# A new order for the same 1682 steps: memory attention mixed with a state-space convolution on one core

## The chip, the core and the metric

The kernel runs on one core of a Trainium2 chip. The core has five engines that matter here, each with an instruction list of its own that it works through strictly in order: PE (TensorE, the matmuls), ACT (ScalarE), DVE (VectorE), POOL (GpSimd) and SP (SyncE, which does nothing here but issue transfers). An engine stops at an instruction until everything that the instruction waits for has been signalled by the other engines or by a transfer. The metric is the time of one execution in microseconds (us) of the device. Data is bf16.

## The reference, cut to what matters

One input x, 2048 tokens of 512 features, goes through two branches, and a gate per token mixes them:

```
# branch A: 32 heads of 16, 4 segments of 512 tokens
for s in range(4):
    p     = softmax(qs @ ks^T / 4 + causal mask)        # inside the segment
    a_dot = p @ vs
    a_mem = (phi(qs) @ M) / (phi(qs) @ z + 1e-6)        # from the segments before
    o_s   = sigmoid(beta) * a_mem + (1 - sigmoid(beta)) * a_dot
    M    += phi(ks)^T @ vs;  z += sum(phi(ks))          # phi(t) = t+1 if t>0 else exp(t)
a = concat(o_s) @ wo
# branch B: K[d,l] = Re sum_n C[d,n] * exp(dt*A[d,n]*l) * (dt*B[d,n]);  causal convolution
b = irfft(rfft(pad(x)) * rfft(pad(K))) + x * Dskip
g = sigmoid(sum(x * gate_w))
out = g * a + (1 - g) * b
```

## The kernel before, in words

**Work.** The kernel is a list of 1682 steps, and a step is one vector or scalar instruction, one transfer, or a group of matmuls that belong together. Branch A is worked in 16 groups: 4 segments times 4 groups of 8 heads (`project`, `scores`, `ophase`). A group has five score tiles of 128x2048 or 128x1024, so there are 80 in all. For each, PE writes the scores into PSUM banks 0 to 3 (line 1108), ACT takes the exponential into SBUF (line 1132), and PE multiplies the result with the values. In the first two segments PE adds the causal mask as a matmul (line 1127), in the last two DVE multiplies by it (line 1145). `norm` (lines 1092 to 1099) divides by the sums. The score tiles all use the same four banks, so the scores of one tile cannot begin before the exponential of the one before has ended. All other results of PE go through the four banks 4 to 7, or through 0 to 3 between two score tiles.

**The convolution.** `ssm_prep` and `ssm_powers` compute exp(dt*A) and its squares up to the power 2^9 (ACT squares on line 824, copies from line 832). `tables` builds for each of four blocks of 128 features, in complex products on DVE (lines 1228, 1231, 1235 and `cmul1`), two tables of powers; the lag matmuls (line 1284, eight steps per table, named 1027 to 1030 and 1032 to 1035 for table 0, with the copies 1031 and 1036) make the convolution kernel K from them. The convolution itself is a transform in two levels: `x_level1` (steps 1215 to 1298) multiplies x by a 128-point transform and stores the result to DRAM, scr_Z, through a few SBUF tiles; `tail` reads it back, 2 halves times 16 frequencies, and multiplies it with the transform of K. `finals` adds both branches in PSUM, applies the gate in the last copy and stores the output.

**Copies.** Every result in PSUM that a later matmul needs is copied to SBUF. Most copies go through `S.evac` (line 224), which has two forms: ACT (line 226, or 229 with a factor) and DVE (227, or 230 with a factor). Which engine makes a copy is written in the order. There are 243 steps with such a choice.

**Queues.** Nearly all transfers are issued by SP, in its list's order (line 222, and line 724 for the transposing loads of x, steps 577 and 794 for segments 2 and 3). An issue occupies SP for a few tenths of a microsecond, a transposing one for longer. A step that issues a transfer waits on SP for its data, and the transfers behind it wait too.

**What sets the order.** The order of all steps is written out in full, in the string `ORDER` (lines 372 to 456). Each word is a step's number, then `a` where a copy goes to ACT (`v` or nothing: DVE), then the slots (PSUM banks or buffer numbers) that the tiles which begin their life there take:

```
1027/4/0      # step 1027 (first lag product of table 0); PSUM choice 4, buffer 0 of its pool
1240v         # step 1240, a copy, on DVE
```

For a tile of one bank the choices 0 to 7 stand for the banks 4, 5, 6, 7, 0, 1, 2, 3. `replay` (line 235) walks the words and appends each step to its engine's list; `emit` (line 264) then puts in the waits that the data and the reuse of buffers need, given that order. So one word in another place changes the lists of one engine, and the waits, but no instruction.

**Steps that the prediction names.** Start: 23 (an 8 KB load of beta), 36 (first exponential of `ssm_prep`), 189 (exponential of the gates, line 885). `x_level1`: 1217, 1219, 1222, 1224, 1240, 1250, 1253, 1255 (copies into the tiles that are stored to scr_Z), 1225, 1235, 1251 (stores). 106 is a square of `ssm_powers` (line 824), 157 and 175 are copies of a power to bf16 (line 832), 987, 1044, 1099 and 1102 copies of powers into the tables 0, 1 and 2 (line 226 or 227). 801 is the copy of a projection of segment 3. 1657 to 1664 are the last two output tiles.

Of the kernel before, what the change touches and what calls it, by code (L numbers as in the profile page):

```python
# [372 lines left out]
16/0 386/0 214/0 193/0 205/1 15/0 10/0 17/0 0/0 25/1/0 11/1 9/2 27/2 33/0 26 41/0 44/1 45 28 34/2 42/3 12/3 35/4  # L373
29/3/1 46 47 30a 1236/0 7/0 1239/0/0 1249/4/1 23/0 37/5 183/0 38 39 189/0 190 36/6 191 43/7 48/0 54/8 3/0 40 194 50/9
1240v 49/10 13/4 53/1 59/1 51/11 52 5/0 60/5 178/2 14/5 1250a 55/12 66/3 64/0 65 58/0 56/13 57 61a/0 62/1 63v 72/4
76/1 77/5 78 67a/0 68 91v/1 79v/2 31/6/2 32a 90/6 70/2 71 181/3 192/0 1247/2 1237/7 1238a 92 88/0 89 102/7 103v/3
1248a 82/1 83/1 184/2 104 100/0 80 101 1/0 19/0 200/3/0/0 201a 202 115v/4 292/0/1/1 84 293a 116 179/1 114/3 294 182/0
20/0 18/0 203/4/0 204a 22/0 372/0 180 208/1 209a 210/2 222/0/0 4/0 217/3/0/0 218 220 223 1215/1 212/0 112/0 113 186/3
213a 69 94/1 211a 373/1 127v/5 187 983v/0 374/0 206/0 185 224 207a 794/0 1251 1221/2/1 1222v 987v/0 128 8/0 219 126/5
1223/1 1224a 124/0 225/0/0 93 81 984v 105 991/0 992 125 988/1 986v 195 226 227 1241 136/3 138/6 137 96/2 139v/6 993  # L380
989 990 251/0/2/2 985v 252a 196/2 197 216 95 140 254/1/1 253 150/7 255a 117 151v/7 1225 998/0 387/3 388v 129 229/0/1
215 230 24 148/2 149 1218/0/0 1219a 231 1231/1/1 1232a 1233/0 1234v 381/2/2 1235 997 163v/8 237/0/2 238 999 106/0 239
389/1 390v 164 152 162/0 1001/1 994 108/3 141 375/0 228/3 232 233 234/0 241/0/0 242 198 199/0 382a 243 295/0/0 1216/2
1217a 1220 263/0/1 264 160/3 265 1252/1/1 1253a 296v 995/0 165 1000 161 153 1002 240/2 1254/0 1255a 244 270/0/1 188
271 996 272 245 795/1 796 172v/9 1256 235 236/0 393/0 266/0/0 267 394a 1003 246/1 268 1007/1 1006 247 1004/0 107 248
378/1/0/0 1008 379a 1244/3/0 1245a 278/0/2 279 280 1226/0/1 173 1005 174 269/1 273 1227a 274 275/2 1010/1 1009 276
1012 277/1 1242/3 1278/0 1243a 1246 385/0 1228/2 282/0/0 283 284 334/0/1 335a 309/0/1 310 1229a 1230 311 281/3 1011
1018 1019/0 1016/1 1020 221/0/0 256/2/0/0 257 259 258 1021 1013/0 331/1/2/2 332a 302/0/0 303 304 285 286 305/0/0 287/3
306 1015 288 118/1 119/5 260 577/0 307 261/0 1289/1/0 1281/2/1 317/0/2 318 1282a 289 1014 1022/0 1023 377/1 1024 1290a
319 1257/1 1025/0 120 1017 1026 132/6 1291/2 1292a 1047/1 1293 308/0 249/3 250a/0 380 297/1/0/0 312 313 314/4 1049/0  # L390
321/0/0 322 323 1046 333 315 435/2/1/1 1279/3 1027/4/0 1028 1280a 1029 1030 436a 1265/3/0 320/2 324 325 1263/5 130/2
131 437 316/0 298 300 299 1283 383/0 142/3 143/7 144 326/5 156/0 327 1032/0 384 1033 1034 1035 328 1050 262 1266a
1031a 154/0 1264a 155 1036a 1040/0 1037 343/0/1 1044v/0 73a/3 344 1038 1045v/0 1041a 1051 1042v 1055 1048 1056/0
1260/1/1 1267 1043a 6/0 345 350/0/1 1261a 109v/2 169a/0 1053/1 1057 1052 1058 351 352 1059/0 1054 85a/4 110 1060
1065/1 86 1064 170 1066 1061 1067 1068/0 1070 290/3 291a 74 1069 1258/2 1259a 1062/1 1076 1262 1063 1077/0 329/0
1273/1/0 346/0/0 347 348 1275/3 1276a 438/2/0 439a 362/0/2 363 330a 364 1268/3/1 1274a 1277 1269a 1270/2 349/0 353 354
355/0 358/0/0 359 360 87 1073 1078 356 1079 357/1 1080/1 391/1 1039 402/0/0 403 392a 395 1271a 1272 301/3 336/1/0/0
404 337 338 339 1074/0 361/2 1081 1071/1 405/0/1 145a/1 1075 1082 406 111 407 1083/0 171 1296/0/0 1297a 1072 340 166/1
75 365 366 396 409/0/0 410 411 408/1 133a/5 1084 483/0/2/2 397/4/0/0 398 400 399 367/1 134 1286/5/1 1294/6 1295a 1298
121a/6 122 123 157a/8 368 158 369 168/2 1105/1 1107/0 1284/7 1285a 1104 341 1108 167 146 412 175v/7 1287a 1288 159 413  # L400
1090/6/1 1091 1092 1093 1094a 401/2/1 417/0/2 418 135 484a 97a/9 98 443/0/0/0 444 414/2 176 99 177 485 445 147 446 415
342 419 416/0 1085/3 1086 1087 1088 1109/0 1103a 1114/0 1089a 1299/0 453/0/0 1097 454 455 1300/0 1098 1113 1307/1
1106/0 1115 1096 447 448 1116 1101a 486/0/1 1095 1100a 1306/1 1117/1 1099v 370/1 1118 421/0/1 1102a 1110 422 423
532/3/2 487a 529/2/0/0 1120/0 533a 450/0/1 1119 451 452 530a 420/0 1129/1 424 1121 425 426/3 371a 1317/2 1128 1301/3/0
1336/0 1132/0 1302a 1130 496/0/0 497 498 1303/2/0 1304a 1305/0 457/0/1 458 459 1310/1/1 1311a 578/3 579 1308/2/1 1309a
1312/1 1318/1 580 465/0/2 1111/1 466 427 456/1 460 467 461 1313/1/0 1314a 469/0/0 470 1112 428 471 1122 1324/0
# [1101 lines left out]
```

## Time and profile before

| | |
|---|---|
| median of 3 runs | 294.76 us (294.18, 294.76, 295.40) |
| the profiled execution | 294.76 us |
| its span in the profile | 293.0 us, mean granted TensorE clock 0.988 |
| PE busy | 254.9 us, 87% of the span |
| DVE busy | 257.9 us, 88% (641 instructions) |
| ACT busy | 254.0 us, 87% (314 instructions) |
| POOL busy | 5.2 us |
| weight loads on PE (overlapping) | 174.3 us |
| 80 exponentials of the scores (line 1132) | 137.0 us of ACT, 1713 ns on average |
| chain that ended last | PE 53%, ACT 30%, DVE 8%, issue 4%, DMA 3% |
| DMA | 41.83 MB, 143 GB/s on average; the queue that SP feeds took 49.3% |

The span is what the profiler saw of the execution, and the time is longer by what lies around it. Busy time counts an engine's instructions, not its waits. In a row of the timeline stand the start in us, the duration in us (of the whole run of equal instructions, where several stand together), the engine, the line of the code, the operation, the tiles and the form; in brackets the idle time of the engine ahead of it and what ended that idle time. "SPq" is SP's queue, "issue" idle time in which the engine waited for nothing that the profile shows. In a table by stretches each row gives a stretch of time, its length, then for each engine the busy time and how many instructions began in it, the granted clock of TensorE and what the transfers took. In the chain of waits a row gives only start, duration, engine, tile and line.

### The profile page before, as it was taken

Reading aid. Unit: us, or ns where it says so; the run is one execution under the profiler, and the core shown is the slowest. Engines: PE = TensorE matmul, PEld = TensorE weight load, DVE = VectorE, ACT = ScalarE, POOL = GpSimd, SP = SyncE. Lnnn points to the kernel's source line nnn. Section 1 sums busy time; section 2 is a strip of 40 time slices with the busy share of each in tenths; the row PEclk is TensorE's granted clock in tenths of the full one; section 3 lists DMA queues with packets and bytes.
Section 4 is the critical chain, followed back from the end, with each engine's and each line's share of the span. In section 5 each row is a group of like instructions: output and inputs, shape, how many; then the busy total and the mean of one; then the engine's idle time right before and its main releaser. Section 6 shows DMA issues by size and latency. Waiting matters only on the chain.

```text
span 293.0 us, 12663 instructions
## 1 busy us (share of the span) xinstructions
PE 254.9 (87%) x5623; PEld 174.3 (59%) x5665; DVE 257.9 (88%) x641; ACT 254.0 (87%) x314; POOL 5.2 (2%) x11
## 2 busy tenths in 40 slices
PE   3677888776777889999999979999999999999993
PEld 2333364546345657677777757777767777646662
DVE  3998999999999998999999969889988899787643
ACT  3998999998999999989999869898998899987630
POOL 5000000000000000000000000000000000000000
PEclk9999999999699999999999999999999999999999
DMA  6999331941314455506526546547657766421135
GB/s 178 305 175 196 86 102 39 213 123 41 92 53 103 120 142 169 192 21 199 153 76 189 135 157 171 201 142 237 207 158 218 223 192 204 130 74 40 38 74 144
DMA packets 45128, 41.83 MB, mean 143 GB/s; under 512 B 21009, under 2 KB 40466, under 8 KB 45074
## 3 DMA queue, kind: packets, MB, share of 16 engines
q1 hardware_dynamic: 43922, 40.47, 49.3%
q8 instruction: 44, 0.72, 1.0%
q10 hardware_dynamic: 1152, 0.56, 0.8%
q14 instruction: 10, 0.08, 0.1%
HBM read 25.88 MB, written 6.29 MB: 110 GB/s over the span
## 4 chain that ended last, share of the span: by engine, by line
PE 53%; ACT 30%; DVE 8%; issue 4%; DMA 3%; SPq 0%; ACTq 0%
PE psum L692 52%; ACT sb L1132 15%; ACT sb L226 9%; ACT sb L824 2%; DMA scr_Z<-sb 2%; DMA sb<-in_B_B_im_dram 1%; ACT sb L832 1%; DVE sb L1228 1%; DVE sb L1235 1%; DVE sb L1348 1%; DVE sb L1231 1%; ACT sb L983 1%; DVE sb L1099 1%; DVE sb L227 1%; DVE sb L1145 1%
## 5 line engine op out<-in xcount | busy, mean ns | idle before, releaser
L692 PE MATMUL psum<-sb 128*32 128x20 bf16 (+17 forms) x5535 | 248.2, 218 | 28.8 <-ACT sb L1132 11.2
L692 PEld LDWEIGHTS psum<-sb 128*128 128x128 bf16 (+8 forms) x5577 | 167.7, 99 | 106.4 <-issue 24.9
L1132 ACT ACTIVATE sb<-psum 128x2048 bf16<-128x2048 f32 (+1 forms) x80 | 137.0, 1713 | 12.4 <-PE psum L692 11.9
L226 ACT ACTIVATE sb<-psum 128x512 bf16<-128x512 f32 (+3 forms) x143 | 87.6, 651 | 9.9 <-PE psum L692 7.0
L227 DVE CAST sb<-psum 128x512 bf16<-128x512 f32 (+2 forms) x44 | 31.1, 715 | 7.6 <-PE psum L692 5.5
L1235 DVE TENSOR_TENSOR sb<-sb 128x512 bf16<-128x512 bf16 (+3 forms) x44 | 30.4, 698 | 0.2
L1231 DVE TENSOR_TENSOR sb<-sb 128x512 bf16<-128x512 bf16 (+3 forms) x44 | 30.4, 695 | 0.2
L1228 DVE TENSOR_TENSOR sb<-sb 128x512 bf16<-128x512 bf16 (+3 forms) x44 | 30.3, 696 | 0.0
L1348 DVE TENSOR_TENSOR sb<-sb 128x1024 bf16<-128x1024 bf16 x32 | 21.7, 686 | 2.2 <-ACT sb L226 2.0
L1145 DVE TENSOR_TENSOR sb<-sb 128x512 bf16<-128x512 bf16 (+1 forms) x40 | 18.1, 472 | 2.1 <-ACT sb L1132 2.0
L1099 DVE TENSOR_TENSOR sb<-psum,sb 128x256 bf16<-128x256 f32 x32 | 13.5, 421 | 0.4
L230 DVE TENSOR_SCALAR sb<-psum,sb 128x512 bf16<-128x512 f32 x9 | 6.7, 748 | 6.3 <-PE psum L692 6.2
L824 ACT ACTIVATE sb<-sb 128x512 f32<-128x512 f32 x18 | 11.4, 640 | 0.0
L229 ACT ACTIVATE sb<-psum,sb 128x512 bf16<-128x512 f32 x6 | 4.1, 686 | 6.2 <-PE psum L692 6.2
L1096 DVE RECIPROCAL sb<-psum 128x16 f32<-128x16 f32 x32 | 8.1, 253 | 1.3 <-PE psum L692 1.2
L1182 DVE TENSOR_TENSOR sb<-psum,sb 128x512 bf16<-128x512 f32 x12 | 8.3, 689 | 0.3
L1038 ACT ACTIVATE sb<-sb 128x512 bf16<-128x512 bf16 x12 | 7.7, 642 | 0.5 <-PE psum L692 0.4
L825 DVE TENSOR_TENSOR sb<-sb 128x256 f32<-128x256 f32 x18 | 7.6, 420 | 0.3 <-ACT sb L824 0.3
L983 ACT ACTIVATE sb<-psum 128x512 bf16<-128x512 bf16 x12 | 7.3, 610 | 0.3 <-PE psum L980 0.3
L826 DVE SCALAR_TENSOR_TENSOR sb<-sb 128x256 f32<-128x256 f32 x18 | 7.5, 416 | 0.0
L1097 DVE TENSOR_TENSOR sb<-sb 128x16 f32<-128x16 f32 x32 | 5.5, 172 | 0.4
L832 ACT ACTIVATE sb<-sb 128x512 bf16<-128x512 f32 x9 | 5.6, 635 | 0.0
(79 smaller groups left out, 116.8 us busy)
## 6 DMA issues: line engine op xcount, KB each, us to landing
sb<-c_DNM SPq DMA_DIRECT2D x32, 480.0 KB, 4.1
scr_Z<-sb SPq DMA_DIRECT2D x16, 256.0 KB, 2.9
sb<-scr_Z SPq DMA_DIRECT2D x32, 128.0 KB, 3.5
sb<-sb SPq DMA_DIRECT2D x32, 128.0 KB
sb<-in_A_x_dram SPq DMA_DIRECT2D x5, 512.0 KB, 5.0
sb<-sb SPq DMA_DIRECT2D x20, 64.0 KB, 3.2
out_dram<-sb SPq DMA_DIRECT2D x18, 64.0 KB, 1.8
sb<-sb SPq DMA_DIRECT2D x8, 136.0 KB, 3.8
```

Of the source, the lines that this page charges most:

```text
L226: fa = lambda e: e.activation(dst(), src(), ACT.Copy)
L227: fd = lambda e: e.tensor_copy(dst(), src())
L692: mm = lambda e, o_, l, r_, st, sp, **kw: e.matmul(o_, lhsT=l, rhs=r_, start=st, stop=sp, skip_group_check=True, **kw)
L824: op("ACT", ("As", 512), lambda e, sq=sq, Z=Z: e.activation(ap(sq, n=512), ap(Z, n=512), ACT.Square), r=[Z], w=[sq], key=PW[h] + PWS * k)
L983: op("ACT", ("Ax", 512), lambda e: e.activation(ap(ek, n=512), ap(P, n=512), ACT.Exp), r=[P], w=[ek])
L1099: op("DVE", ("V1", 256), lambda e: e.tensor_tensor(ap(o1, gi * 16, [[128, 4], [32, 4], [1, 16]]), ap(T, dims=[[68, 4], [17, 4], [1, 16]]), ...
L1132: o = op("ACT", ("Ax", 4 * w), lambda e, P=P, pT=pT, w=w: e.activation(ap(pT, dims=[[w, 4], [1, w]]), ap(P, dims=[[512, 4], [1, w]]), ACT. ...
L1145: op("DVE", ("V2", 1024 if ent is None else 512), lambda e, pT=pT, pd=pd, md=md: e.tensor_tensor(ap(pT, dims=pd), ap(pT, dims=pd), md(), A ...
L1228: op("DVE", ("V2" if n > 1 else "V1", 256 * n), lambda e: e.tensor_tensor(run(tile, ne, dst, 1), run(tile, ne, src, sstep), ap(pw, cl * 51 ...
L1231: op("DVE", ("V2" if n > 1 else "V1", 256 * n), lambda e: e.tensor_tensor(run(t2, n, 0, 1), run(tile, ne, src, sstep), ap(pw, cl * 512 + 2 ...
L1235: op("DVE", ("V2" if n > 1 else "V1", 256 * n), lambda e: e.tensor_tensor(D_(), D_(), ap(t2, n * 128, [[-n * 128, 2], [2 * n, 64], [1, 2 * ...
L1348: op("DVE", ("V2", 1024), lambda e, Y=Y, X=X, K3=K3: e.tensor_tensor(ap(Y, dims=[[512, 2], [256, 2], [1, 256]]), ap(X, dims=[[256, 2], [0, ...
```

## The change

Only the string `ORDER` is changed. The 1682 steps, their instructions, transfers, tiles and the memory for them are the same. The order of the words is another nearly everywhere, made from the old one by many small moves; on average a step stands 2 places from its old one in PE's list, 7 in ACT's, 10 in DVE's and 5 in SP's. 44 of the 243 copies change their engine: 28 go from DVE to ACT and 16 from ACT to DVE, so that ACT has 331 steps in place of 319 and DVE 629 in place of 641. Tiles take other slots here and there. The 80 exponentials stand in the same order as before.

Of the diff, which replaces all 83 lines of the string, these are the lines that hold the steps of the prediction (before, then after; whole lines):

```
...
-29/3/1 46 47 30a 1236/0 7/0 1239/0/0 1249/4/1 23/0 37/5 183/0 38 39 189/0 190 36/6 191 43/7 48/0 54/8 3/0 40 194 50/9
-1240v 49/10 13/4 53/1 59/1 51/11 52 5/0 60/5 178/2 14/5 1250a 55/12 66/3 64/0 65 58/0 56/13 57 61a/0 62/1 63v 72/4
...
-213a 69 94/1 211a 373/1 127v/5 187 983v/0 374/0 206/0 185 224 207a 794/0 1251 1221/2/1 1222v 987v/0 128 8/0 219 126/5
-1223/1 1224a 124/0 225/0/0 93 81 984v 105 991/0 992 125 988/1 986v 195 226 227 1241 136/3 138/6 137 96/2 139v/6 993
-989 990 251/0/2/2 985v 252a 196/2 197 216 95 140 254/1/1 253 150/7 255a 117 151v/7 1225 998/0 387/3 388v 129 229/0/1
-215 230 24 148/2 149 1218/0/0 1219a 231 1231/1/1 1232a 1233/0 1234v 381/2/2 1235 997 163v/8 237/0/2 238 999 106/0 239
...
-1217a 1220 263/0/1 264 160/3 265 1252/1/1 1253a 296v 995/0 165 1000 161 153 1002 240/2 1254/0 1255a 244 270/0/1 188
...
-306 1015 288 118/1 119/5 260 577/0 307 261/0 1289/1/0 1281/2/1 317/0/2 318 1282a 289 1014 1022/0 1023 377/1 1024 1290a
...
-321/0/0 322 323 1046 333 315 435/2/1/1 1279/3 1027/4/0 1028 1280a 1029 1030 436a 1265/3/0 320/2 324 325 1263/5 130/2
-131 437 316/0 298 300 299 1283 383/0 142/3 143/7 144 326/5 156/0 327 1032/0 384 1033 1034 1035 328 1050 262 1266a
-1031a 154/0 1264a 155 1036a 1040/0 1037 343/0/1 1044v/0 73a/3 344 1038 1045v/0 1041a 1051 1042v 1055 1048 1056/0
...
-121a/6 122 123 157a/8 368 158 369 168/2 1105/1 1107/0 1284/7 1285a 1104 341 1108 167 146 412 175v/7 1287a 1288 159 413
...
-1106/0 1115 1096 447 448 1116 1101a 486/0/1 1095 1100a 1306/1 1117/1 1099v 370/1 1118 421/0/1 1102a 1110 422 423
...
-619 620 628/0/1 629 535 536/0 621/1 543 605 645 694/0/0/0 695v 627/1 800/2/1/1 801v 630 606 607 622 696 623/0 663/0/2
...
-1622 1623v/2 962 966 1665/3 1657/0 970 1641/2 1669/4 976/3/1/1 963/1 967/1 971 972 1642 1658 1670 977 978 979 1666
-973/2 974 1643a 1653 1654 1655 1656 975 980 981/5 982a 1610/6 1659 1660v/3 1671 1667 1672/4 1673 1668a 1678 1679 1680
-1681 1601/1 1630/2 1602 1603v/5 1631 1632a 1633 1634 1635 1636 1611 1612v 1613 1614 1615 1616 1661/7 1662 1663 1664v
-1674 1675 1676 1677
+15/0 16/0 0/0 10/1 23/0 9/5 11/3 17/5 33/0 25/4/1 189/0 190 26 34/13 12/2 41/5 1236/1 27/0 37/0 28 35/10 36/1 38 7/0
...
+1250a 183/2 193/0 53/7 52 47 1240a 19/0 178/3 64/3 1237/6 66/1 1247/3 65 54/9 62/1 1238a 192/0 4/0 60/2 20/0 18/0
...
+136/3 1251 81 218 227 219 215 1221/0/1 229/0/0 220 137 148/3 388v 230 991/1 293a 389/3 129 1241 983v 216 24 1233/1/0
+140 984v 992 231 1222v 1223/2 72/1 381/0/1 1224a 184/2 294 987a/0 390v 237/0/2 150/5 1234v 238 151v/6 149 70/0 989/0
+577/0 386 993 382a 1231/2 375 228/3 232 233 71 234/5 254/0/2 988 1225 235 794/0 163v/8 187 239 1232a 1235 241/0/0 82/3
...
+995/1 378/3/2/0 999 996 296v 1255a 265 1216/0/0 96/4 270/0/1 271 1218/1 1253a 240/2 244 245 95 1217a 161/3 272 266/0/0
+267 1219a 1256 379a 268 162 1006 1228/0/1 1226/1 1007/0 393/3 278/0/2 246/0 394a 172v/9 1008 1227a 153 141 279 269/3
...
+256/0/0/0 1003 1278/1 1021 331/3/0/1 1230 106/1 1005 107 311 1012 302/0/0 120/6 332a 383/0 303 796 1246 257 304
...
+333 435/2/1/2 1050/1 314/0 1046/0 130/0 298 436a 322 315 323 1047 1283 1049 1027/3/1 132/0 1028 1293 1029 1030 1031a
+1032/2 316/1 300 1033 1034 131 1035 1036a 343/0/1 344 1051/0 1045v 1037/0 1042v/0 1041a 1260/3/0 320/0 1038 1044a
+1258/2 142/2 324 299 109v/7 325 97a/5 1263/1/1 1048 1055 98 99 73a/3 144/2 326/5 1043a 345 350/0/1 1264a 351 110 1259a
+74 1056/1 327 143 1057 328 1052 1265/1 111 1040 352 1053/1 346/0/0 157v/1 1058 347 1054 1059/0 1064 158 1065/1 156/3
...
+1102a/0 1336/1 448 1115 455 421/0/0 422 487a 1100a 1301/1/0 342 423 171 529/3/2/0 1116 450/0/1 1117/0 168 1118 424
+1302a 1306/2 1106 451 1120/0 371a 1101a 1096 452 1119 456/1 1095 1098 1307/0 1308/2/1 1129/1 1309a 425 1128 496/0/0
+497 1097 175a/6 1303/2/1 1318/0 498 426/4 457/0/0 530a 1304a 1121 458 459 532/3/1 1099a 1130 1310/2/0 1311a 1305/0
...
+615/3 1394a 619 1469/3 449 620 628/0/1 694/0/1/0 621/0 629 800/1/2/2 622 626 801a 627/2 1451/2 1444/0 607 1396/1
+663/0/2 623/0 664 695v 1206/3 697/0/1 630 631 632 696 667/0/0 1462/1 1407/2 802 1207 1208 1209 698a 571/0/3/0 1387 809
...
+1681 1630/5 1678 1679 1631 1632a 1611 1612v/3 1636 1635 1602 1603v 1613 1615 1661/0 1657/1 1614 1658 1616 1662 1659
+1634 1633 1660v/4 1663 1664a 1674 1677 1676 1675
```

129 lines of the change are left out of this document (64 added, 65 removed).

## The prediction, made before the time of the changed kernel was known

> **What bounds the kernel now.** I read the page's first lines, then the busy time by stretches, then the timeline with what ended each idle time.
>
> ```profile
> span 293.0 us, 12663 instructions
> PE 254.9 (87%) x5623; PEld 174.3 (59%) x5665; DVE 257.9 (88%) x641; ACT 254.0 (87%) x314; POOL 5.2 (2%) x11
> ```
>
> The sum is made on this execution: 294.76 us, span 293.0 and 1.76 us around it. It is also the median of the three runs (294.18 to 295.4). No engine is full over the whole, so I cut the span where the limit changes:
>
> ```profile
> core 0: us, PE busy (x) PEld busy (x) DVE busy (x) ACT busy (x) POOL busy (x), PEclk, DMA share, GB/s
> 7.28:25.05 17.77, 12.31 (x110) 6.65 (x112) 17.08 (x51) 17.71 (x35) 0.00 (x0) 1.00 1.14 228
> 25.05:41.12 16.07, 13.04 (x187) 6.33 (x189) 14.61 (x49) 14.99 (x22) 0.00 (x0) 1.00 0.44 117
> 41.12:118.68 77.56, 61.92 (x1711) 42.38 (x1724) 75.38 (x177) 74.90 (x98) 0.66 (x1) 0.96 0.39 109
> 110.00:118.68 8.68, 8.66 (x193) 6.57 (x192) 7.70 (x14) 7.85 (x9) 0.00 (x0) 1.00 0.42 140
> 118.68:170.00 51.32, 50.00 (x1233) 36.67 (x1238) 50.30 (x119) 47.63 (x60) 0.67 (x1) 1.00 0.47 141
> 170.00:180.00 10.00, 8.40 (x311) 5.66 (x311) 7.54 (x24) 7.07 (x8) 0.00 (x0) 1.00 0.49 163
> 180.00:285.00 105.00, 103.12 (x2000) 73.09 (x2015) 88.23 (x217) 88.50 (x94) 0.00 (x0) 1.00 0.51 154
> 285.00:293.00 8.00, 3.47 (x70) 1.90 (x69) 2.25 (x3) 0.69 (x1) 0.00 (x0) 1.00 0.55 145
> ```
>
> From 7.28 to about 110 ACT and DVE are both full while PE has holes. From 110 on PE is full: 8.66 of 8.68 us, then 50.00 of 51.32, 8.40 of 10 and 103.12 of 105, in all 4.8 us of holes. The last 8 us are the tail. So a reorder gains where ACT idles before 110, or in those 4.8 us; elsewhere it moves cover about.
>
> **The change, term by term.** Instructions and transfers are the same; 44 copies out of PSUM or between tiles change engine, 28 from DVE to ACT and 16 back. PE's list hardly moves: steps stand 2 places from before on average, DVE's 10, ACT's 7. The 80 exponentials keep their order, so they serve as marks, and I compare what each list holds ahead of a mark.
>
> *Start, to the first exponential of head group 1 (41.09).* ACT's list ahead of it exchanges three steps for three (1217, 1219, 106 out; 1240, 987, 1255 in), about half a microsecond each: no change in work. What changes is the waiting.
>
> ```profile
> 18.93 3.69 SPq L724 DMA_TRANSPOSE sb<-in_A_x_dram  x1
> 22.66 0.59 SPq L222 DMA_DIRECT2D scr_Z<-sb  x1
> 22.66 4.75 DMA scr_Z<-sb
> 27.50 0.60 ACT L226 ACTIVATE sb<-psum 128x512 bf16<-128x512 f32 x1 [0.94 <-DMA scr_Z<-sb]
> ```
>
> The store 1251 stands behind a transposing load (794) on SP's queue, lands at 27.4, and only then may ACT overwrite its tile. In the new list 794 stands after the store, and copy 1224 stands after two more exponentials. The 0.94 us goes. Against it, the 8 KB load 23 is now issued ahead of the loads that release PE's transposes (line 771), one issue later (0.43 us for one as small), and ACT's copy at 7.28 waits for those transposes:
>
> ```profile
> 3.72 0.43 SPq L222 DMA_DIRECT2D sb<-in_A_beta_dram  x1
> 7.28 1.02 ACT L226 ACTIVATE sb<-psum 128x1024 bf16<-128x1024 bf16 x1 [1.61 <-PE psum L771]
> ```
>
> Two short steps (189, line 885, and the first exponential of the preparation, 36) move into that wait, which pays for the issue. ACT's table loads stay three.
>
> The transposing loads have a price on SP's queue.
>
> ```profile
> L724 SPq DMA_TRANSPOSE sb<-in_A_x_dram x3: 2653/3687/6498, 10.5 to 54.5; - x3
> ```
>
> 577 (moved 155 places up) issues while the next store on SP, 1225, waits for copy 1224 anyway. 794 stands between 1225 and store 1235, whose tile copy 1217 overwrites. From the end of 1224 SP needs 0.59 + 3.69, and 4.75 to land, 9.0 us; ACT has 9.7 us of work (14 steps at their own durations) ahead of 1217. That covers it, by 0.7; at the longest issue, 6.50, ACT waits 2.8 - 0.7 = 2.1. Value 0, bounds 0 and +2.1.
>
> The start's own term is -0.9; bounds -1.6 (the rest of the 1.08 us idle between 25.05 and 41.12, and half the wait at 7.28, go too) and +0.4 (the late load is not covered).
>
> *Short slots between exponentials.* All scores share four PSUM banks, so after an exponential PE needs 0.74 us for the next scores, and ACT idles if it holds less other work than about 0.8 us:
>
> ```profile
> 57.85 0.74 PE psum L692 x12
> 45.68 1.88 ACT L1132 ACTIVATE sb<-psum 128x2048 bf16<-128x2048 f32 x1 [0.17 <-PE psum L692]
> 58.61 1.88 ACT L1132 ACTIVATE sb<-psum 128x2048 bf16<-128x2048 f32 x1 [0.30 <-PE psum L692]
> 102.26 1.88 ACT L1132 ACTIVATE sb<-psum 128x2048 bf16<-128x2048 f32 x1 [0.18 <-PE psum L692]
> 63.24 0.98 ACT sb L226 x2
> ```
>
> Ahead of these three stands one copy (0.49) and a little, or 0.75 us. The new list has two steps, about 0.95 to 1.1 us, in each, and no slot before 110 under 0.8; what fills them came from slots of 1 us and more. Term -0.6 (the three idle times), bounds -0.65 and 0.
>
> *Lag products of table 0 (line 1284).*
>
> ```profile
> 66.04 1.19 PE L692 MATMUL psum<-sb 128*32 128x20 bf16 x128 [0.94 <-ACT sb L1132]
> 70.87 1.93 PE L692 MATMUL psum<-sb 128*32 128x20 bf16 x110 [1.24 <-issue]
> 71.70 0.44 ACT L226 ACTIVATE sb<-psum 128x320 bf16<-128x320 f32 x1 [0.77 <-PE psum L692]
> 61.47 1.77 ACT sb L1132
> 69.06 0.57 PE psum L692 x54
> 70.87 0.80 PE psum L692 x73
> ```
>
> Their first PSUM tile is a bank of the scores, so they start only when an exponential ends (0.94), and the second half's copy makes ACT wait 0.77. The new slots are banks 7 and 6, the eight pieces stand together behind the last scores of group 2, and they can run under that exponential (the 1.77 at 61.47). The 1.24 us stall in PE's own issue may stay. Term -0.5, bounds -0.8 and +0.6 (the copies 1036 and 1031 now stand directly behind that exponential, and the eight pieces take 1.19 + 0.57 + 0.80 us in the rows and the chain even without the stall, ahead of its 1.77).
>
> *Copies given to ACT while ACT is the limit.* Ahead of the exponential at 102.26 the new list adds 1240, 987, 1044 and 1102 and drops 157:
>
> ```profile
> 72.57 0.77 ACT L226 ACTIVATE sb<-sb 128x256 bf16<-128x256 bf16 x2
> 77.34 0.52 ACT sb L832
> ```
>
> 0.49 + 3 x 0.39 - 0.52 = +1.1; with part of the next two (175, 1099) before PE takes over at 110, I take +1.2. Bounds 0 (DVE is as full as ACT there, and has 1.1 us less ahead of 118.68) and +1.9 (both in full).
>
> *PE-bound part, 110 to 285.* PE's total is fixed; only its 4.8 us of holes can go. One shows what the engine changes do:
>
> ```profile
> 170.48 0.69 DVE L227 CAST sb<-psum 128x512 bf16<-128x512 f32 x1 [0.47 <-PE psum L692]
> 171.09 0.41 DVE L1145 TENSOR_TENSOR sb<-sb 128x512 bf16<-128x512 bf16 x1
> 171.52 2.02 PE L692 MATMUL psum<-sb 128*128 128x512 bf16 x52 [0.16 <-DVE sb L1145]
> 174.91 3.32 PE L692 MATMUL psum<-sb 16*128 16x192 bf16 x113 [1.36 <-issue]
> ```
>
> The mask at 171.09 stood behind copy 801, for which DVE had itself waited. The new list gives 801 to ACT, into a slot that held nothing. But the larger hole behind it, 1.36 us, is PE's issue and is not touched. With 28 copies off DVE and its list shorter, I take a quarter of 4.8: -1.2; bounds -3.4 (all but that 1.36) and +4.1 (second rival).
>
> *Tail.* The products of 1657 and 1658 move behind the last wait as filler, and the last copy goes from DVE to ACT:
>
> ```profile
> 286.62 0.69 ACT L229 ACTIVATE sb<-psum,sb 128x512 bf16<-128x512 f32 x1 [1.89 <-PE psum L692]
> 288.66 0.75 DVE L230 TENSOR_SCALAR sb<-psum,sb 128x512 bf16<-128x512 f32 x1 [0.86 <-PE psum L692]
> ```
>
> 0.75 - 0.69 = -0.1, bounds -0.2 and +1.0 (ACT issues four stores between these two copies, and could be late for the last).
>
> Sum: -0.9 - 0.6 - 0.5 + 1.2 - 1.2 - 0.1 = -2.1: **292.7 us**, span about 291.
>
> **Rivals.** *More than the sum.* The lead of the start survives to 110 because DVE, as full as ACT there, has less ahead at nearly every mark, and PE's holes close but for the 1.36. For it: DVE's list ahead of the table ends is 1 to 2 us shorter for tables 0 to 2. Against: issue stalls do not depend on order. -0.9 - 0.6 - 0.8 + 0.6 - 3.4 = -5.1: 289.6.
>
> *The terms cancel.* Slots that were harmless become short once the pace shifts, and the quarter of the holes does not come: without it and with copies at +1.9 the sum is -0.2, 294.6.
>
> *Slower: ACT late where PE is the limit.* Place: the scores of segment 2.
>
> ```profile
> 189.05 1.88 ACT L1132 ACTIVATE sb<-psum 128x2048 bf16<-128x2048 f32 x1 [0.89 <-PE psum L692]
> ```
>
> The new ACT list holds 5.3 us more ahead of this exponential than the old one (each step at its own duration), PE's 1.1 less. ACT idles 51.32 - 47.63 = 3.7 us from 118.68 to 170 and 2.9 in the next ten, 6.6 together, and while these can be used nothing is lost. They are waits for PE, though; if they stay where they are, the extra 5.3 replaces the +1.2 of the sum: +4.1, 296.8. It decides from the point where ACT's extra work exceeds the idle time it can reach.
>
> *A second stretch at half clock.*
>
> ```profile
> 71.94:78.76 6.82, 5.08 (x39) 2.61 (x39) 6.82 (x20) 6.58 (x12) 0.00 (x0) 0.50 0.23 63
> ```
>
> Right after the lag products of table 0 PE was granted half its clock for 6.82 us, while ACT set the pace. The products of table 2 (near 128 to 133), split in two before, now stand as eight pieces in a row, in the part where PE is the limit. A repeat there costs half of 6.82: 292.7 + 3.4 = 296.1. Against: tables 1 to 3 brought none. [...]
>
> **How the numbers follow.** The forecast's own case, 292.7 within about 1.5 either way, has 0.42, more than the sum 0.22, cancelling 0.15, late ACT 0.15, half clock 0.06. Half a percent is 1.5 us, about what a measurement of this kernel tells from no change, so faster means under 293.3 and slower over 296.2. Faster: 0.28 of the forecast's case, 0.22, and 0.01 of cancelling: 0.51. Slower: 0.03 + 0.15 + 0.04 = 0.22. Same: 0.27. The range reaches a little past both outer cases, 288.2 to 298.4; the forecast's own is 291.2 to 294.2.
>
> **What would show it.** Right: ACT has no wait on scr_Z before 41; the first exponential of head group 1 starts about 0.9 earlier; ACT's idle time from there to the exponential now at 118.68 falls from 2.7 to under 1.7; PE's holes from 110 to 285 are under 4. Wrong: ACT waits of a microsecond at the lag copies; PE waiting for L1132 from 180 on by more than now; a granted clock under 1 after 110; or a start that is later.

## The result, and the profile after

The changed kernel takes **303.92 us** (median of 4 runs, 300.73 to 304.9), the kernel before 294.61 us on the same chip (294.18 to 295.4). The ratio is 1.029, with a 95% interval of 1.021 to 1.038: slower by 9.3 us, where 292.7 was forecast. The profiled execution took 303.2 us, with a span of 301.4. Ratios here and below leave out runs in which the chip was disturbed (six of ten for the new order in the "fat" form below, three of four for the new order with the old engines), so a median and its ratio need not match to the last digit.

The first lines of the page of the changed kernel, and the engine shares of its chain of waits:

```profile
span 301.4 us, 12708 instructions
PE 264.1 (88%) x5665; PEld 177.3 (59%) x5665; DVE 250.9 (83%) x629; ACT 258.8 (86%) x326; POOL 5.2 (2%) x11
PE 59%; ACT 25%; issue 7%; DVE 5%; DMA 4%; SPq 0%
```

The same line of the chain before the change:

```profile
PE 53%; ACT 30%; DVE 8%; issue 4%; DMA 3%; SPq 0%; ACTq 0%
```

DVE is relieved and ACT has more to do, as the 44 copies that changed engine would have it. PE's busy time is 9.2 us higher, but these two figures can't be compared: the trace of before holds only 5,623 of the 5,665 matmuls (all 42 that are missing have 512 columns), and in a variant of the old order whose trace holds them all (the first of the three forms "further apart" below) PE is busy for 262.3 of 292.7 us. What can be compared is "issue": it went from 4% of 293.0 to 7% of 301.4, some 9 us more of the chain in which the engine waited for nothing that the profile names.

The exponentials have one order in both kernels, so I cut both spans at the same six of them. Busy time by these stretches, before:

```profile
41.09:92.22 51.13, 39.23 (x1041) 26.21 (x1052) 50.06 (x118) 49.59 (x64) 0.66 (x1) 0.93 0.37 100
92.22:107.94 15.72, 12.56 (x434) 8.40 (x432) 15.59 (x45) 15.50 (x24) 0.00 (x0) 1.00 0.46 122
107.94:124.29 16.35, 15.39 (x350) 11.38 (x348) 15.34 (x28) 15.45 (x21) 0.00 (x0) 1.00 0.53 171
124.29:139.63 15.34, 15.01 (x446) 11.66 (x446) 14.77 (x46) 13.08 (x23) 0.00 (x0) 1.00 0.34 107
139.63:266.36 126.73, 123.17 (x2617) 87.97 (x2631) 113.58 (x270) 113.84 (x120) 0.67 (x1) 1.00 0.55 166
266.36:293.00 26.64, 21.58 (x446) 14.10 (x449) 14.41 (x33) 11.36 (x13) 0.00 (x0) 1.00 0.32 81
```

And after, between the same exponentials:

```profile
38.46:92.26 53.80, 42.12 (x1031) 26.29 (x1029) 50.00 (x120) 49.95 (x67) 0.00 (x0) 0.87 0.28 86
92.26:114.81 22.55, 18.03 (x491) 11.90 (x491) 18.32 (x44) 16.33 (x25) 0.66 (x1) 0.77 0.45 134
114.81:129.99 15.18, 14.70 (x310) 10.53 (x307) 12.87 (x26) 15.18 (x19) 0.00 (x0) 1.00 0.33 99
129.99:148.04 18.05, 15.25 (x449) 11.67 (x447) 15.00 (x44) 14.32 (x29) 0.00 (x0) 1.00 0.34 104
148.04:275.43 127.39, 124.68 (x2636) 88.09 (x2634) 110.76 (x269) 115.72 (x121) 0.68 (x1) 1.00 0.53 164
275.43:301.40 25.97, 22.25 (x448) 13.80 (x446) 12.61 (x30) 12.69 (x15) 0.00 (x0) 0.99 0.33 83
```

The columns are the stretch, its length, the busy time of PE, weight loads, DVE, ACT and POOL, the granted clock and the transfers. The start gives 2.6 us (38.46 for 41.09), the long middle takes 2.7 of that back, and two stretches cost the rest: the one that holds the lag products of table 1 takes 22.55 us instead of 15.72, at a mean clock of 0.77 instead of 1.00, and the one with those of table 2 takes 18.05 instead of 15.34 at full clock. From 148 on the two kernels run side by side (127.39 and 126.73), and the tail is 0.7 shorter.

In both places PE stops by itself. Its timeline after the change, around the lag products of tables 0, 1, 2 and 3:

```profile
63.66 3.59 PE L692 MATMUL psum<-sb 128*128 128x512 bf16 x247
69.65 3.03 PE L692 MATMUL psum<-sb 128*32 128x20 bf16 x110 [2.40 <-issue]
...
100.18 1.18 PE L692 MATMUL psum<-sb 32*128 32x448 bf16 x60
102.78 2.72 PE L692 MATMUL psum<-sb 128*32 128x20 bf16 x128 [1.42 <-issue]
108.00 8.19 PE L692 MATMUL psum<-sb 128*128 128x512 bf16 x149 [2.50 <-issue]
...
133.84 1.87 PE L692 MATMUL psum<-sb 128*32 128x20 bf16 x207 [0.17 <-DVE sb L1235]
138.34 3.22 PE L692 MATMUL psum<-sb 128*32 128x20 bf16 x105 [2.63 <-issue]
...
182.95 3.35 PE L692 MATMUL psum<-sb 128*32 128x20 bf16 x115 [1.11 <-issue]
```

Ahead of the stops at tables 0 and 2 stand 247 matmuls in 3.59 us and 207 in 1.87. Each matmul has a weight load of its own (5,665 of each on the page), so that is 400 to 500 instructions. At table 1 the eight pieces stand four and four, as before the change; new there is step 578 right behind them, 16 matmuls of one column for the gate. The five stops are 10.1 us together. Before, the stops at the same products were 1.24, 0.75, none and 1.36.

What ends them is not in the table of waits, but it is in the transfers. The page counts the packets of a queue of the kind "instruction" while the program runs, the same for both kernels:

```profile
q8 instruction: 44, 0.72, 1.0%
```

In the packet records each of the 44 has 16,384 bytes (0.72 MB together); they begin between 24 and 290 us, and 11,330 matmuls and weight loads over 44 are 257 per packet, an estimate that takes the queue to be PE's. These are the packets beside the stops, from the packet records of the two traces (us):

```
after:   packet  67.03 +1.34    PE goes on at  69.65, 1.28 after its end   (stop 2.40)
after:   packet 100.36 +0.88    PE goes on at 102.78, 1.54 after its end   (stop 1.42)
after:   packet 105.68 +0.94    PE goes on at 108.00, 1.38 after its end   (stop 2.50)
after:   packet 135.47 +1.45    PE goes on at 138.34, 1.42 after its end   (stop 2.63)
after:   packet 180.50 +0.95    PE goes on at 182.95, 1.50 after its end   (stop 1.11)
before:  packet  68.52 +1.10    PE goes on at  70.87, 1.25 after its end   (stop 1.24)
before:  packet  97.61 +1.30    PE goes on at 100.24, 1.33 after its end   (stop 0.75)
before:  packet 172.69 +0.88    PE goes on at 174.91, 1.34 after its end   (stop 1.36)
```

In all eight PE resumes 1.25 to 1.54 us after a packet of instructions has landed. Over the profiles of all fifteen kernels of this document, 37 of the 38 idle times of PE of 0.5 us or more that "issue" ended were over 1.21 to 1.64 us after such a packet. So "issue" is read here as PE having run out of instructions: the profile names no releaser, and the reading rests on these times and, below, on the runs with few instructions. That gives theory S (supply), to be tested: a group of matmul steps that uses up instructions faster than the packets bring them stops PE, and stretches at half clock follow. The rival, theory W (waits), puts the loss on the copies and transfers that were moved.

### The profile page after: what moved, and what is told of

Same layout as the page of the kernel before. It is cut to its first block, busy times and chain, and to the rows that moved or that the text cites. A ratio compares the mean times of both kernels' runs of the same rounds, so it can differ in the third digit from the quotient of the medians.

```text
span 301.4 us, 12708 instructions
## 1 busy us (share of the span) xinstructions
PE 264.1 (88%) x5665; PEld 177.3 (59%) x5665; DVE 250.9 (83%) x629; ACT 258.8 (86%) x326; POOL 5.2 (2%) x11
## 4 chain that ended last, share of the span: by engine, by line
PE 59%; ACT 25%; issue 7%; DVE 5%; DMA 4%; SPq 0%
PE psum L692 58%; ACT sb L1132 11%; ACT sb L226 9%; DMA sb<-c_DNM 3%; ACT sb L824 2%; DVE sb L1228 1%; DVE sb L1235 1%; DMA sb<-in_A_beta_dram 1%; ACT sb L832 1%; DVE sb L1231 1%; PE psum L980 1%; ACT L908 0%; SPq L222 0%; ACT sb L983 0%; DVE sb L787 0%
## 5 line engine op out<-in xcount | busy, mean ns | idle before, releaser
L692 PE MATMUL psum<-sb 128*32 128x20 bf16 (+19 forms) x5577 | 258.0, 221 | 31.8 <-ACT sb L1132 12.4
L692 PEld LDWEIGHTS psum<-sb 128*128 128x128 bf16 (+8 forms) x5577 | 170.3, 100 | 115.7 <-issue 38.3
L226 ACT ACTIVATE sb<-psum 128x512 bf16<-128x512 f32 (+3 forms) x149 | 91.7, 655 | 14.4 <-PE psum L692 13.7
L227 DVE CAST sb<-psum 128x512 bf16<-128x512 f32 (+2 forms) x38 | 27.1, 718 | 6.8 <-PE psum L692 6.5
L229 ACT ACTIVATE sb<-psum,sb 128x512 bf16<-128x512 f32 x8 | 5.3, 684 | 7.2 <-PE psum L692 7.1
L1249 DVE TENSOR_TENSOR sb<-sb 128x256 bf16<-128x256 bf16 x8 | 3.2, 405 | 7.0 <-PE psum L692 7.0
L230 DVE TENSOR_SCALAR sb<-psum,sb 128x512 bf16<-128x512 f32 x7 | 5.2, 750 | 4.7 <-PE psum L692 4.7
L226 ACT ACTIVATE sb<-sb 128x256 bf16<-128x256 bf16 x14 | 6.1, 461 | 3.2 <-PE psum L692 3.2
```

Of the source, the lines that this page charges most:

```text
L226: fa = lambda e: e.activation(dst(), src(), ACT.Copy)
L227: fd = lambda e: e.tensor_copy(dst(), src())
L692: mm = lambda e, o_, l, r_, st, sp, **kw: e.matmul(o_, lhsT=l, rhs=r_, start=st, stop=sp, skip_group_check=True, **kw)
```

## The experiments

**The old order with the lag products packed.** Only 11 matmul steps of PE move; engines, copies and transfers stay as before. PE's list around tables 0, 1 and 2:

```
-1027 1028 1029 1030 1265 320 324 325 1263 1032 1033 1034 1035 343
+1265 320 324 325 1263 1027 1028 1029 1030 1032 1033 1034 1035 343
...
-1090 1091 1092 1093 401 417 418 443 1085 1086 1087 1088 453
+1090 1091 1092 1093 1085 1086 1087 1088 401 417 418 443 453
...
-1143 1144 1145 1148 1146 1337 429 1331 593 495 537 1149 1150 1151 583
+1143 1144 1145 1148 1146 1149 1150 1151 1337 429 1331 593 495 537 583
```

> The old order and the old engines, with only the lag products of tables 0, 1 and 2 put eight in a row (11 matmul steps of PE moved). Theory S: PE stalls by its own issue for 2 us or more at each of them (before: 1.24, 0.75 and none), more time at half clock than the 6.8 us of before, and 297 to 302 us. Theory W: 294 to 296 us.

Measured: 306.63 us (303.3 to 308.14), ratio 1.036 (1.027 to 1.046). Eleven steps of PE in another place cost as much as the whole change (the intervals overlap). From its timeline, at tables 0 and 2:

```profile
71.87 2.52 PE L691 MATMUL psum<-sb 128*32 128x20 bf16 x110 [2.62 <-issue]
...
137.60 4.72 PE L691 MATMUL psum<-sb 128*32 128x20 bf16 x76 [2.63 <-issue]
```

The stops of 2.62 and 2.63 us are of the size of the changed kernel's (its line numbers are lower by one). At table 1 it was only 0.79, so "2 us or more at each of them" was missed there, and the time lies over the 302 expected at most for S. The time at half clock came as expected and more, 30.7 us in place of 6.8. W's 294 to 296 is excluded.

**The old order with only table 2 packed** (the last of the three edits above alone).

> The old order with the lag products of table 2 alone put eight in a row (steps 1149, 1150, 1151 moved up behind 1146), where PE is the limit and there is other work enough for it. Theory S: a stall of about 2.6 us by PE's own issue appears there (none before), the time rises by 2 to 4 us, 297 to 299 us. If PE makes the stall up behind it: 294 to 296 us.

Measured: 298.43 us (297.25 to 299.58), ratio 1.012 (1.006 to 1.017). Before the change, where table 2's products stand five and three:

```profile
125.83 5.09 PE L692 MATMUL psum<-sb 128*128 128x256 bf16 x209
131.08 1.31 PE L692 MATMUL psum<-sb 128*128 128x512 bf16 x11 [0.16 <-issue]
...
132.54 0.92 PE L692 MATMUL psum<-sb 128*32 128x20 bf16 x96
```

With the eight in a row:

```profile
125.81 3.52 PE L692 MATMUL psum<-sb 128*128 128x256 bf16 x230
131.37 2.45 PE L692 MATMUL psum<-sb 128*32 128x20 bf16 x74 [2.05 <-issue]
```

209 matmuls in 5.09 us bring no stop, 230 in 3.52 us one of 2.05. Up to the exponential at 124.2 the two runs differ by 0.1 us; behind it this one is 2.4 later, in a place where nothing else is moved. A second loss of 2 us comes at table 3, which was not touched: its stop grew from 1.36 to 1.91, and 3.4 us at half clock stand beside it.

**The new order with the lag products split again.** PE's list after the edit has other steps between the halves of tables 0 and 2, and the gate matmuls 578, which stood right behind those of table 1, go 16 steps of PE further back:

```
-1030 1032 1033 1034 1035 343 344 1260 320 1258 324 325 1263
+1030 343 344 320 324 325 1032 1033 1034 1035 1260 1258 1263
...
-1151 1143 1144 1145 1146 1331 429
+1151 1331 429 1143 1144 1145 1146
```

> The new order, with the lag products of tables 0 and 2 in two halves again, other PE steps between the halves (for table 0 the steps 343, 344, 320, 324, 325, for table 2 the steps 1331 and 429), and the gate matmuls 578 moved away from behind those of table 1. Theory S (PE runs out of instructions at eight lag pieces in a row, and the holes bring on stretches at half clock): the idle times of 2.4 and 2.6 us that end with PE's own issue at tables 0 and 2 fall under 1.3 each, the half-clock time falls well under 24 us, and the time is 296 to 301 us. Theory W (the loss is waits for the copies and transfers that were moved): PE's order is beside the point, 302 to 305 us.

Measured: 302.1 us (301.46 to 302.65), ratio 1.024 (1.016 to 1.032). At table 0 the stop fell from 2.40 to 0.49:

```profile
69.76 1.02 PE L692 MATMUL psum<-sb 128*32 128x20 bf16 x107 [0.49 <-issue]
```

At table 2 none of 0.2 us or more is left, and the stretch there takes 17.15 us instead of 18.05. At table 1, without 578 behind it, 0.38 and 0.46 us took the place of the stop of 2.50, and the stretch takes 18.15 us instead of 22.55. But the time hardly moved, and by its bounds this run goes to W. The gain at table 1 was lost right behind it: the next stretch takes 18.27 us instead of 15.18. The chain at its start holds a load from scr_Z, a wait of the kind that W names, and behind it 4.84 us of PE, most of them at half clock (114.54 to 117.96); what each of the two costs was not taken apart.

```profile
109.36 3.24 DMA sb<-scr_Z
```

The longest stretch at half clock, 17.1 us in a row from 70.17 to 87.24, cost little by comparison: DVE and ACT are the full engines there, not PE, and from the exponential at 58.39 to the one at 88.86 it takes 30.47 us, where the changed kernel takes 30.09 with 10.2 us at half clock.

```profile
70.17:87.24 17.07, 12.99 (x195) 6.37 (x185) 15.96 (x42) 15.82 (x22) 0.00 (x0) 0.50 0.23 62
```

**The new order with the old engines** for all 44 copies.

> The new order, with all 44 copies on the engines that they had before. Theory W in its form 'ACT has too much to do': under 300 us. Theory S: PE's list is that of the changed kernel, so the stalls stay, and 302 to 306 us.

Measured: 323.47 us, from 314.92 to 325.17, without an interval, so only the sign is used: even the fastest run is 10 us over the slowest of the changed kernel. The list order and the engines belong together. W in the form "ACT has too much to do" is wrong, since giving the copies back makes it worse. S did not foresee this size either; it was not followed up.

**Holes of PE filled, in the new order.** Three single matmuls of the first transform level are repeated; the result is the same.

```
+FILL = {(9, 0): 6, (9, 1): 8, (12, 1): 5}
-lambda e, ...: mm(e, ap(P, n=512), ...)
+lambda e, ..., n=FILL.get((b4, hf), 1): [mm(e, ap(P, n=512), ...) for _ in range(n)][-1]
```

> The changed kernel, with three matmuls of the first transform level (steps 1281, 1263, 1265) done 5, 6 and 8 times over with the same result, so that PE is busy in holes of 1.1, 1.2 and 1.8 us in which it waited for exponentials at 58, 73 and 75 us. If the half clock is a cause by itself: the stretches at half clock at 62 (3.4 us) and 76 (10.2 us) go or shrink, the first exponential tile B0 of segment 1 starts at least 1.5 us earlier than in the changed kernel (92.26), and the time is 300 to 302 us. If the half clock only goes along with waits that are there anyway: that exponential within 0.5 us of 92.26, and 303 to 305 us.

Measured: 306.55 us (304.15 to 308.03), ratio 1.039 (1.031 to 1.047): 2.6 us over the changed kernel by the medians, with intervals that overlap. The stretch at 62 is gone, but another one begins at 68.97, right behind the stop at table 0:

```profile
62.19:65.60 3.41, 2.72 (x159) 1.90 (x160) 3.41 (x11) 3.41 (x6) 0.00 (x0) 1.00 0.25 82
68.97:75.80 6.83, 6.83 (x123) 3.73 (x108) 5.32 (x20) 4.12 (x9) 0.00 (x0) 0.50 0.17 37
```

So the fillers did not keep the clock up across a stop for instructions, and brought no gain. Neither reading's numbers came.

**The lag products with few instructions.** Four kernels keep every step, wait, copy and engine of the two orders, but a lag step has two matmuls of 320 columns in place of 32 of 20: 4 instructions, not 64. Once on the whole array ("fat"), once on 32 columns of weights as the lag products use it ("few_low"). The convolution kernel K is then not computed.

```
-for sl in range(sl0, sl0 + 4):
-    for cc in range(2):
-        for dq in range(4):
-            i = mm(e, ap(P, sl * NF, n=NF, p0=32 * dq, np_=32), ap(G, ..., [[2, NG]]), ap(F, ..., [[2, NF]]), ...)
+for _ in range(2):                                  # fat
+    i = mm(e, ap(P, n=320), ap(G, n=128), ap(F, n=320), True, True)
...
+for _ in range(2):                                  # few_low, dq = sl0 // 4
+    i = mm(e, ap(P, n=320, p0=32 * dq, np_=32), ap(G, n=32), ap(F, n=320), True, True, tile_position=(0, 32 * dq))
```

> The changed kernel with each lag step (32 matmuls of 20 columns on a 32x32 part of the array, 64 instructions with their weight loads) replaced by two matmuls of 320 columns on the whole array (4 instructions, about as long). The lag products, and with them the convolution kernel, are not computed; all steps, waits and copies stay. Theory S (instruction supply and the half clock that follows on it): no idle time ended by issue at the lag steps, little half clock after 55 us, and 295 to 298 us, within 2 us of the old order with the same replacement. Theory R (the new order also has longer waits for copies and exponentials of its own): the gap of 9 us between the two orders stays at 5 us or more.

> The old order with the same replacement of the lag steps (the convolution kernel is not computed). The base for the run before this one. Theory S: its own small stalls (1.24, 0.75 and 1.36 us) and its 6.8 us at half clock go as well, 290 to 293 us. If the old order loses nothing there: 294 to 295 us.

> The changed kernel with each lag step replaced by two matmuls of 320 columns on the same narrow part of the array as before (32 columns of weights): 4 instructions in place of 64, and the array as little used as by the lag products. The convolution kernel is not computed. If the number of instructions is what costs: as with the wide replacement, 289 to 297 us, and no idle time ended by issue at the lag steps. If the narrow use of the array (and the half clock after it) is what costs: 299 us or more.

> The old order with each lag step replaced by the two narrow matmuls of 320 columns (the convolution kernel is not computed): the base for the same replacement in the new order (290.3 us). If the whole loss of the new order hangs on the lag instructions: 290 to 292.5 us, not faster than the new order. If the new order also loses elsewhere: under 288 us.

Measured:

| lag steps | new order | old order |
|---|---|---|
| as they are | 303.92 us, ratio 1.029 (1.021 to 1.038) | 1 |
| fat | 290.9 us (288.86 to 291.76), ratio 0.986 (0.981 to 0.992) | 291.08 us, ratio 0.989 (0.983 to 0.995) |
| few_low | 290.32 us, ratio 0.986 (0.980 to 0.992) | 291.46 us, ratio 0.987 (0.984 to 0.990) |

(These are the four runs of the fat new order on which its ratio rests; all ten ran from 288.86 to 296.91, with a median of 294.35.) With few instructions in the lag steps the two orders are equal, so theory R's gap of 5 us or more did not come, and the fat new order lies lower than S had it (295 to 298). By the medians the new order pays 13.6 us for the lag instructions and the old one 3.3 (294.79 beside those runs), by the ratios 12.8 and 3.9: the difference, 8.9 to 10.3 us, is the whole loss. Cut at the same six exponentials as above, few_low saves the new order 2.7, 6.1, 0, 3.1 and 2.4 us in the first five stretches and the old order 0, 0.1, 0.7, 0.6 and 2.2. So the orders differ where the tables 0, 1 and 2 stand.

Four lag steps take 1.19 us as they are (without a stop), 1.26 in the fat form and 0.47 in few_low. So the fat form keeps the time on PE, and few_low the narrow use of the array. Both gain the same, so it is the number of instructions that costs. Two expectations were missed. The half clock did not go: few_low has 13.7 us of it in the new order (from 56.84, 70.49 and 80.73) and 10.2 in the old, without any stop for instructions, so it also comes without such stops. And one idle time ended by issue is left behind table 1, 2.2 us after a packet and so of another kind, whose cause is open:

```profile
103.45 11.01 PE L692 MATMUL psum<-sb 128*64 128x256 bf16 x249 [1.33 <-issue]
```

The page of few_low in the new order:

```profile
span 287.1 us, 10750 instructions
...
q8 instruction: 37, 0.61, 0.9%
```

That is 1,958 recorded instructions fewer than in the changed kernel; 38 of them are matmuls that this trace lacks, and 1,920 (32 lag steps, 60 each) are really gone, with 7 packets: 274 for each packet. The stretch of table 2 takes 14.92 us there (18.05 in the changed kernel), that of table 1 16.41 (22.55), both at full clock:

```profile
89.56:105.97 16.41, 12.69 (x249) 8.29 (x251) 16.17 (x43) 15.80 (x24) 0.65 (x1) 1.00 0.60 183
121.16:136.08 14.92, 13.78 (x208) 9.74 (x207) 14.82 (x44) 14.09 (x30) 0.00 (x0) 1.00 0.43 122
```

**The new start in front of the old order.** The first 292 words of the new order, then all other steps as before.

> The first 292 words of the new order, up to the second exponential of head group 1 (step 280), with their engines, and behind them all other steps in the old order on the old engines (lag products as before). Theory S: the loss comes from the lag products, so 293 to 295 us, with the gain of the start kept in part. If the start itself brings the loss on (transposing loads beside the stores, tables later): over 297 us.

Measured: 302.8 us (300.6 to 304.17), ratio 1.028 (1.020 to 1.036). The lead of the start is there (40.45 at the second exponential tile of head group 1, 42.96 before), and 6.7 us are lost between that tile and 58.02 (53.88 before), at the seam. What the new start had put off stands ahead of everything else there. So this says nothing on S; it shows that a part of one order can't be set before a part of another.

**The old order with the lag products further apart**, in three forms, looking for a kernel faster than both orders. First the next scores (343, 344) between the halves of table 0, with copies 1031 and 1264 ahead of them and the exponential 345 ahead of copy 1036; then also table 3's last four steps one by one; then the first form with two fillers against the half clock.

```
-1030 1265 320 324 325 1263 1032 1033 1034 1035 343 344        # PE, all three
+1030 1265 320 324 325 1263 343 344 1032 1033 1034 1035
...
-620 628 694 627 800 663 1206 1207 697 631 632 667 1208 1209   # PE, second form
+620 1206 628 694 1207 627 800 1208 663 697 1209 631 632 667
...
+FILL = {(11, 0): 6, (15, 1): 4}                               # third form
```

> The old order with one thing changed: the scores of the next tile (steps 343, 344) and their exponential go ahead of the second half of the lag products of table 0, so that the halves stand further apart. Theory S: the stall of 1.24 us there falls under 0.6, and 292.5 to 294.3 us. If the stall was hidden behind ACT's copies: 294.3 to 295.5 us.

> The old order with the lag products pulled apart further: of table 0 as in the run with the scores between its halves, of table 3 its last four steps (1206 to 1209) one by one between the steps 620, 694, 800 and 697. Theory S: the stall of 1.36 us at table 3 goes too, and 292.5 to 294.3 us, faster than both kernels. If PE's stalls there are made up by less waiting behind them: 294.3 to 296 us.

> The old order with the scores between the lag halves of table 0 (295.1 us, stretches at half clock at 75.5 for 3.4 us and at 89.2 for 10.2 us in its profile), and two matmuls of the first transform level done over with the same result: 1273 six times, ahead of a hole of 1.3 us at 74, and 1296 four times, ahead of one of 0.5 us at 88. If the half clock is what eats the gain of the wider halves: both stretches go, and 292 to 293.8 us, faster than both kernels. If not: the time stays at 294.5 to 296 us, or more by the 1.7 us that the fillers take.

Measured: 295.08, 296.7 and 295.16 us; ratios 1.001 (0.998 to 1.004), 1.005 (1.001 to 1.008) and 1.001 (0.998 to 1.003). In the first the stop at table 0 is gone (no idle time ended by issue there, 1.24 before), and the first exponential of segment 1, at 85.28, is 1.0 us further ahead of before than the first one of head group 1 was. Then the clock is halved for 10.2 us and the lead is gone:

```profile
89.18:99.42 10.24, 10.24 (x260) 6.84 (x259) 9.27 (x28) 7.93 (x13) 0.65 (x1) 0.50 0.28 80
```

The third form has no such stretch there. From the first exponential of segment 1 to the fourth after it, it takes 14.78 us (86.03 to 100.81), the first form 17.75 (85.28 to 103.03), the kernel before 14.71: by these profiles, one of each, the 10.2 us at half clock had cost 3.0. It then lost 1.6 us against the first form at table 3, with a stop of 1.68 us (1.36 in the first form) and 3.4 us at half clock beside it. Three of its twelve runs had a mean clock of 1.000 and took 293.94 to 295.21. In the second form a stop of 1.26 us at table 3 stayed, and the time lies over both its readings. Nothing that was tried beats the kernel before.

## Why the prediction was wrong, step by step

**The step that failed** is the term of the lag products, -0.5 with bounds -0.8 and +0.6. It saw the eight pieces of table 0 side by side, asked only what runs beside them, and let the stop of 1.24 us "stay" at its size; tables 1 and 2 had no term in the sum. The reasoning that went with it, "issue stalls do not depend on order", is false: eleven steps of PE's list in another place turned stops of 1.24 us and none into 2.62 and 2.63. The row was on the table (1.24 us, ended by issue, in the middle of 110 lag matmuls), and so was the row that spoke against packing: table 2, with its pieces split five and three, had no such stop. By the runs with few instructions the term, over all tables, is worth +8.9 to +10.3 us.

Packing is not the whole of it. The largest loss, 6.8 us, is at table 1, whose pieces stand as they did. The new order with its lag products split gave back 4.4 us of it, with 578 moved away (other steps moved too), and eight pieces in a row cost only 0.79 us of stop there in the old order. What else decides there was not shown.

**The half clock** was given 0.06, at table 2 and at +3.4. It came behind table 1 and in the stretches before: by the trace's record of the clock 23.9 us up to 115, in place of 6.8. Of the 6.8 us lost at table 1, the stops take 2.0 (1.42 + 1.37 on the chain, less 0.75), and the other 4.8 are an estimate, an upper one, for the 10.2 us at half clock there.

```profile
101.36 1.42 issue
...
106.63 1.37 issue
```

The stretches at half clock in the two traces, without the one that the end of the span cuts, last 6.83 us before (from 71.94) and 3.41, 10.24, 3.41 and 6.83 us after (from 62.19, 75.85, 92.91 and 106.57). The longest idle time of PE in the changed kernel from 15 to 115 us, where these four lie, was 2.50 us, and in the kernel before 1.47. What brings the half clock on stays open: no run shows it, and the fillers did not settle it. So that tables 1 to 3 had brought none before was no measure of the chance of a repeat.

**The start** was forecast at -0.9 with a bound of -1.6, by the wait on scr_Z. That wait is gone. All waits of ACT before 41 in the changed kernel:

```profile
ACT L777 <- PEq L1493: 1.7, 1, 1.7
ACT sb L789 <- DVE sb L788: 1.1, 1, 1.1
ACT sb L885 <- DMA sb<-in_A_beta_dram: 0.8, 1, 0.8
ACT sb L762 <- PE psum L758: 0.2, 1, 0.2
```

One profile against one gives -2.6, but two profiles of an identical start differ by up to 1.5. The first exponential of head group 1 starts at 38.42 to 39.31 in six profiles of the new start with its own engines (mean 38.65) and at 39.62 to 41.09 in eight of the old (mean 40.29): -1.6, the bound. The two transposing loads on SP's queue cost nothing, as forecast:

```profile
27.45 3.19 SPq L724 DMA_TRANSPOSE sb<-in_A_x_dram  x1
30.77 0.51 SPq L222 DMA_DIRECT2D scr_Z<-sb  x1
31.32 3.59 SPq L724 DMA_TRANSPOSE sb<-in_A_x_dram  x1
35.01 0.53 SPq L222 DMA_DIRECT2D scr_Z<-sb  x1
```

**Short slots and copies on ACT** (-0.6 and +1.2). The idle times went, but the work that filled them had to come from somewhere. From the first exponential of head group 1 to the seventh after it, before and after:

```profile
41.09:58.61 17.52, 14.57 (x326) 9.38 (x329) 17.45 (x39) 17.00 (x20) 0.00 (x0) 1.00 0.51 129
```

```profile
38.46:57.54 19.08, 15.14 (x334) 9.56 (x333) 19.04 (x45) 19.08 (x26) 0.00 (x0) 1.00 0.40 123
```

ACT's idle time of 0.52 fell to nothing and its busy time rose by 2.1: six more instructions, put off by the start. Most of the lead was a loan. With few lag instructions the new order is ahead by 1.2 us of span (287.08 against 288.26) in one profile of each, but the ratios, 0.986 and 0.987, tell no difference: all other terms together come to about nothing, within a microsecond or two. Their forecast was -2.1 + 0.5 = -1.6.

**PE-bound part** (-1.2): from 139.63 and 148.04 to the same exponential it went the other way by 0.7, with a stop at table 3 in both (1.36 and 1.11). The term was a quarter of 4.8 us of holes, and these were mis-sized: from 110 to 285 the trace of before lacks 22 of 3,748 matmuls, and a matmul that is missing looks like a hole. The first form of the old order "further apart", whose PE list is the old one there, has them all and 2.1 us of holes, 1.36 of them the stop at table 3:

```profile
110.00:285.00 175.00, 172.89 (x3748) 121.76 (x3748) 154.42 (x371) 151.28 (x170) 0.67 (x1) 1.00 0.50 151
```

**Late ACT in segment 2**, the main rival on the slower side, did not come: from the exponential at 139.63 to the one at 189.05 it took 49.42 us before, and 49.26 after. **Tail**: -0.7 in the last stretch of the tables above, -0.1 forecast.

Of the signs named beforehand for being wrong, two came: a granted clock under 1 after 110, and waits of ACT at the lag copies. At table 0 ACT waited 2.53 us for PE's stop to end:

```profile
69.98 0.44 ACT L226 ACTIVATE sb<-psum 128x320 bf16<-128x320 f32 x1 [2.53 <-PE psum L692]
```

ACT's idle time from head group 1 to the exponential that was at 118.68, hoped for under 1.7 us, was not filled but grew: 3.9 + 6.2 us are ACT waiting for PE in the first two rows of the table after.

## What to carry to other kernels

Idle time on PE that "issue" ends can be a shortage, of instructions, as 37 of 38 such times here are read (1.21 to 1.64 us after a packet), and it depended on the order (2.62 us in place of 1.24 at table 0, 2.63 in place of none at table 2): look at how many matmuls stand in the few microseconds ahead of it, and at the packets of the instruction queue. The runs speak for setting matmuls of 20 columns, each with its own weights, in small groups with long matmuls between. At table 0 the runs give a scale: with its two halves of 128 matmuls 0, 1.8, 2.7 and 3.4 us apart, the stop was 2.0 to 2.6, 1.24, 0.49 us and none. At table 2, eight groups of 32 in a row cost 2.0 to 2.7 us of stop, five and three with 3.5 us between them none. A replacement with the same steps and waits but few instructions tells whether instructions or waits set the time. Several profiles of one start are needed before a lead of a microsecond is believed, and the counts of matmuls and weight loads should be compared before a hole of PE is believed.

## What the runs showed of the hardware that was not expected

Instructions arrived during the execution: 44 packets of 16,384 bytes on the queue "instruction" between 24 and 290 us, and 37 in the run with 1,920 fewer instructions of PE (few_low, new order). A packet took 0.88 to 1.45 us beside the eight stops listed above, and PE went on 1.25 to 1.54 us after it had landed. With their weight loads, 247 matmuls in 3.59 us (2.40), 230 in 3.52 (2.05) and 207 in 1.87 (2.63) stood ahead of a stop, its length in brackets, and 209 in 5.09 ahead of none; but at table 1 of the changed kernel 260 in 5.96 us stood ahead of one of 1.42 too, so these figures are no fixed threshold.

Ten microseconds at half clock cost 3.0 us in a stretch where ACT is the fuller engine at full clock (the third form "further apart" against the first, one profile of each), and at most about half of their length at table 1 of the changed kernel (an estimate, from the 4.8 us that the stops there leave). Wider gaps between the lag halves of table 0 removed its stop of 1.24 us and came with a longer stretch at half clock in the same kernel (10.2 us in the first form "further apart", 6.8 before), so a gain at one stop has to be looked for in the whole time.
